# Cells over 24 feed-forward pieces each, and the last two groups of an mLSTM + feed-forward kernel in three float32r parts

## The chip, the cores and the metric

The kernel runs on one core of one Trainium2 chip. The metric is the device time of one execution in microseconds (us), the median of several runs. A core has TensorE (PE, with its weight loads shown apart as PEld), VectorE (DVE), ScalarE (ACT), GpSimd (POOL) and SyncE (SP), which here does nothing but issue DMA transfers. Each engine works through its own instructions in order and waits on semaphores for the others. The profile also shows the queues that issue, for instance SPq.

## The reference

Two blocks follow each other. The first is an mLSTM cell over 4 batches, 8 heads, 768 time steps and a head dimension of 40. The second takes its output as 3072 tokens of 320 numbers through a feed-forward layer of width 2048 with a leaky ReLU.

```python
for t in range(S):
    m_new = np.maximum(f_gate[:, :, t] + m, i_gate[:, :, t])
    f_stab = np.exp(f_gate[:, :, t] + m - m_new)
    i_stab = np.exp(i_gate[:, :, t] - m_new)
    m = m_new
    C = f_stab[..., None, None] * C + i_stab[..., None, None] * np.einsum('bhd,bhe->bhde', vt, kt)
    n = f_stab[..., None] * n + i_stab[..., None] * kt
    h_tilde = np.einsum('bhde,bhe->bhd', C, qt)
    denom = np.maximum(np.abs(nq), 1.0)          # nq = n . q
    y[:, :, t] = o * h_tilde / denom             # o = sigmoid(o_gate)
x = y.transpose(0, 2, 1, 3).reshape(B * S, H * D)
h = x @ w_in                                     # (3072, 320) @ (320, 2048)
return np.maximum(0.01 * h, h) @ w_out           # @ (2048, 320)
```

q, k, v and the gates are float32. w_in and w_out arrive in 64 bits per number, and the kernel turns them into float32 itself.

## The kernel before

**Chunks and groups.** The 768 time steps are cut into six chunks of 128, numbered 0 to 5. A step s is one chunk of one batch: s = 4 x chunk + batch, 24 in all. The recurrence inside a chunk is done with matrix products (scores under a causal mask, and a state per head that goes from chunk to chunk). Chunk g of all four batches gives 512 tokens, and these are group g of the feed-forward. Group g is computed while the cells of chunk g + 1 are computed, so that TensorE always has large matmuls between the small ones.

**A group's 32 pieces** (`ff_units`, L737). The first 16 are eight pairs: the first layer for two blocks of 128 hidden units, five slots of two matmuls (L743), one on the partitions 0 to 63 and one on 64 to 127, 512 columns each, in two PSUM tiles. A pair ends with two leaky ReLUs on ACT (L751), which write into `acts`. The last 16 pieces are the second layer: for each of four blocks of 128 tokens four pieces of four matmuls of 320 columns (L778), then a copy out of PSUM (L786) and an output DMA. All matmuls are float32. The first layer's PSUM tiles and the second layer's `po` share four banks (`psf`), the cells have the other four (`psc`).

**The cells of chunks 2 to 5.** A step has two visits on PE: `u_parts` (scores, and the chunk's addition to the state: L598, L603) and `u_mix` (output: L679). They come for two steps at a time. Behind `u_mix` DVE turns the result (L686), makes denominators, multiplies with the output gate (L690), POOL divides (L693), DVE turns back (L697), and SP stores x to `x_dr` in DRAM (L700). `gather_x` (L703) fetches it from there into `xT`, the input of the group's first layer, with four DMAs for each step. `ahead(s + 2)` then prepares the next step but one: DVE's `prep_kq` (L489, L495), POOL's `prep_vu` (L462) and `state_next` (L576), and SP's loads of k and q for two steps later. The decay matrix `w` is loaded (`spread`), gets the causal mask on POOL (`prep_mask`, L434), and its exponentials are taken on ACT (L442), three for each step in each piece, from three pieces after `ahead` on.

**What sets the order.** PE, DVE, ACT and POOL work in the order in which the program's text issues instructions. The main loop (L945) issues, for each piece, exponentials, masks, the piece, gates of the next chunk, the visits due after it, gathers and loads. `pairs` says after which of the 32 pieces the nine visits of a chunk come, `masks` before which pieces its masks:

```python
masks = {0: (2, 3), 12: (4, 5)}
pairs = (2, 2, 6, 6, 14, 14, 19, 19, 19)
```

SP's DMAs are ordered by the framework. Group 5 runs after the last cells, with nothing beside it.

**Loads of v.** For steps of chunk 1 on, four DMAs of 40 KB put v straight into the tile `S_t` of the batch, which also holds the batch's state (L343).

**Weights.** Eight pieces of w_in and w_out each are loaded in 64 bits and narrowed by `narrow_weights` (L220) on ACT and DVE during chunks 0 and 1. Pool `consts` holds them with all other constants for the whole kernel.

Of the kernel before, what the change touches and what calls it, by code (L numbers as in the profile page):

```python
# [9 lines left out]
F32 = mybir.dt.float32  # L10
U32 = mybir.dt.uint32
U64 = mybir.dt.uint64
AF = mybir.ActivationFunctionType
ALU = mybir.AluOpType
PSUM = bass.MemoryType.PSUM


@with_exitstack
def kernel(
# [28 lines left out]
    P = 128  # L48
# [22 lines left out]
    assert KR == DP and KC == 5 and KC * DP == Dm and GT * 4 <= 2048  # L71

    consts = ctx.enter_context(tc.tile_pool(name="consts", bufs=1))
    gp = ctx.enter_context(tc.tile_pool(name="gates", bufs=1))
    wk = ctx.enter_context(tc.tile_pool(name="wk", bufs=2))
    psf = ctx.enter_context(tc.tile_pool(name="psf", bufs=4, space=PSUM))
    psc = ctx.enter_context(tc.tile_pool(name="psc", bufs=4, space=PSUM))
# [47 lines left out]
    acts = consts.tile([P, NF, GT], F32, name="acts")  # L125
# [36 lines left out]
    QN = NF // 4  # L162
    QC = 4 * P
    WC = KC * 2 * P
    w_in = consts.tile([P, QN, WC], F32, name="w_in")
    w_out = consts.tile([P, NF, Dm], F32, name="w_out")
# [5 lines left out]
    def w_row(r, slot, j):  # L172
        n, e = divmod(j, 2)
        at = (2 * slot + e) * P
        return w_in[DP * r : DP * (r + 1), n, at : at + P]
# [6 lines left out]
    HW = 2 * Dm  # L182
    wide = moe_w_in.dtype == U64
    raws = {}
    if wide:
        raw_t = consts.tile([P, 5 * HW], U64, name="raw")

    def load_weights(n):

        m = n - QN  # L190
        if n < QN:
            dst = w_in[:, n, :]
        else:
            dst = w_out[:, 2 * m : 2 * m + 2, :].rearrange("p a d -> p (a d)")
        to = dst
        if wide:
            if n < 2:
                at = NF * GT - 2 * WC * (n + 1)
                raw = acts_l[:, at : at + 2 * WC].bitcast(U64)
            elif n < QN:  # L200
                raw = raw_t[:, WC * (n - 2) : WC * (n - 1)]
            elif m < 2:
                raw = w_out[:].rearrange("p f d -> p (f d)")[:, (2 + m) * WC : (3 + m) * WC].bitcast(U64)
            else:
                at = (4, 0, 1, 2, 3, 4)[m - 2] * HW
                raw = raw_t[:, at : at + HW]
            raws[n] = (raw, dst)
            to = raw
# [11 lines left out]
    def narrow_weights(n):  # L220
# [3 lines left out]
        if not wide:  # L224
            return
# [102 lines left out]
    def load(s):  # L328
# [12 lines left out]
        for u in range(2):  # L341
            for i in range(2):
                nc.sync.dma_start(  # L343
                    S_v[n][ts(u, SL), u, :, i, :DB],
                    v[b, :, c * P + u * SL : c * P + (u + 1) * SL, DB * i : DB * (i + 1)].rearrange("h p d -> p h d"),
                )
# [43 lines left out]
    def spread(s):  # L390

        c, b = divmod(s, B)
        d = st[s]
        w = wk.tile([P, H, P], F32, name="w", bufs=NL)
        d["w"] = w[:].rearrange("p h t -> p (h t)")[:, : H * SL].rearrange("p (h t) -> p h t", t=SL)
        for u in range(2):
            nc.sync.dma_start(d["w"][ts(u, SL)], a_dr[c, 0, u, b * H : (b + 1) * H, :].partition_broadcast(SL))
# [31 lines left out]
    def prep_mask(s):  # L429
        if s in masked:  # L430
            return
        masked.add(s)
        w = st[s]["w"]
        nc.gpsimd.tensor_tensor(w, w, cm2.unsqueeze(1).to_broadcast([P, H, SL]), op=ALU.add)  # L434
# [31 lines left out]
    def prep_qs(s):  # L466
# [3 lines left out]
        d["qs"] = wk.tile([P, Dm], F32, name="y")[:].rearrange("p (h d) -> p h d", d=D)  # L470
# [232 lines left out]
    def gather_x(s):  # L703

        c, b = divmod(s, B)
        if ("xT", c) not in st:
            st["xT", c] = wk.tile([P, KC, GT], F32, name="xT", bufs=1)
        xT = st["xT", c]
        src = x_dr[s].rearrange("(k p) t -> p k t", p=DP)
        for r in range(2):  # L710
            at = 0
            while at < KC:
                k0, n = run_of(r, at)
                nc.sync.dma_start(xT[DP * r : DP * (r + 1), at : at + n, ts(b, P)], src[:, k0 : k0 + 2 * n - 1 : 2, :])
                at += n

    def u_x(s):
# [3 lines left out]
        if b == 0:  # L721
            st["xT", c] = wk.tile([P, KC, GT], F32, name="xT", bufs=1)
# [14 lines left out]
    def ff_units(g):  # L737
# [36 lines left out]
        def part(n, m):  # L774
# [6 lines left out]
            if m == 3:  # L781
                if n < 2:
                    y = wk.tile([P, Dm], F32, name="y")[:]
                else:
                    y = wk.tile([P, H, D1], F32, name="hn")[:].rearrange("p h d -> p (h d)")[:, :Dm]
# [138 lines left out]
    with tc.manual_schedule(engines={E.PE, E.DVE, E.Activation, E.Pool}):  # L924
# [13 lines left out]
        ffs = ffs[2:]  # L938
# [3 lines left out]
        masks = {0: (2, 3), 12: (4, 5)}  # L942
        pairs = (2, 2, 6, 6, 14, 14, 19, 19, 19)
        now = (None for n in range(2, QN + NF // 2) for _ in narrow_weights(n))
        for c in range(1, NB + 1):  # L945
            if c > 1:
                ffs = ff_units(c - 1)
            cells = cell_units(c) if c < NB else []
            n_ff, n_c = len(ffs), len(cells)
            done = fed = 0  # L950
            waiting = []
            for i in range(n_ff):
                if c == 1:
                    run(now, 2 if i < 10 else 3 if i < 14 else 4)
                    for n in fetch.get(i, ()):
                        load_weights(QN + n)
                    if i == 0:
                        prep_mask(B)
                        ahead(B)
                        load_fi(3)  # L960
# [70 lines left out]
```

## Time and profile before

| what | us |
|---|---|
| median of three runs (527.24, 528.85, 529.04) | 528.85 |
| span of the profiled execution, first to last instruction | 526.4 |
| chunk 0 and group 0 with the cells of chunk 1 | 139.64 |
| group 1 with the cells of chunk 2 | 78.82 |
| group 2 with the cells of chunk 3 | 78.77 |
| group 3 with the cells of chunk 4 | 78.76 |
| group 4 with the cells of chunk 5 | 78.04 |
| group 5, first layer, then second layer | 34.53 + 34.74 |
| from the last matmul to the end | 3.1 |

The stages end where the chain of waits shows the next group's first matmul. The profile has only the span; the run's own time contains some time around it, and the median of the runs lies 2.45 us above the span. The TensorE clock in the profile is the one granted, as a share of the full one.

| engine | busy us | share of the span |
|---|---|---|
| PE | 513.2 | 97% |
| DVE | 240.3 | 46% |
| ACT | 168.1 | 32% |
| POOL | 113.0 | 21% |

Busy times are of the whole span; DVE, ACT and POOL are busy mostly in its first three quarters. "L743" is line 743 of the kernel before.

### The profile page before, as it was taken

To read this page: it belongs to the slowest core of one execution; us is meant where nothing else is said; L and a number is where in the kernel's file an instruction comes from. 1 tells how busy PE (TensorE), PEld (TensorE's weight loads), DVE (VectorE), ACT (ScalarE), POOL (GpSimd) and SP (SyncE) were. 2 spreads that over 40 slices of the span, in tenths; PEclk is the share of its full clock that TensorE was granted. 3 is DMA by queue.
4 is the path that set the end of the run, shared out by engine and by line. 5 is a ranking of instruction groups with operands and counts; after the bars stand their busy time and mean duration, and the time that the engine had idled before them with its cause. 6 is when DMAs were issued, how large, how long until landed. Compare 5 with 4: busy or idle time off the path is not lost.

```text
span 526.4 us, 11333 instructions
## 1 busy us (share of the span) xinstructions
PE 513.2 (97%) x4501; PEld 336.3 (64%) x4501; DVE 240.3 (46%) x431; ACT 168.1 (32%) x458; POOL 113.0 (21%) x145
## 2 busy tenths in 40 slices
PE   8889989999999999999999999999999999999997
PEld 7877878777555577555577555577554577544675
DVE  4679998999328446028445028344028230000000
ACT  4565865534534212034212124212125100122100
POOL 4244354152205121015021015021013010000000
PEclk9668999999999999999999999999999999999999
DMA  9977687888755626685626676626542112000000
GB/s 116 156 204 153 138 212 171 196 145 175 146 137 105 137 72 150 129 174 107 138 75 143 134 150 129 138 76 155 125 102 52 50 52 87 14 0 1 12 12 25
DMA packets 165284, 59.13 MB, mean 112 GB/s; under 512 B 128816, under 2 KB 156016, under 8 KB 165232
## 3 DMA queue, kind: packets, MB, share of 16 engines
q1 hardware_dynamic: 164848, 58.28, 51.0%
q8 instruction: 35, 0.57, 0.5%
q10 hardware_dynamic: 384, 0.13, 0.1%
q14 instruction: 17, 0.14, 0.1%
HBM read 51.68 MB, written 6.70 MB: 111 GB/s over the span
## 4 chain that ended last, share of the span: by engine, by line
PE 83%; SPq 6%; DVE 4%; DMA 2%; ACT 2%; issue 1%; POOL 1%; ACTq 0%; POOLq 0%
PE po L778 38%; PE ph L743 36%; PE pT L679 3%; SPq L213 3%; PE sd L598 3%; SPq L338 2%; SPq L352 1%; PE sd L603 1%; DMA rb<-in_q_dram 1%; DVE raw L245 1%; DVE qn L608 1%; DMA S<-in_v_dram 0%; DMA raw<-in_moe_w_in_dram 0%; PE tk L518 0%; PE hN L649 0%
## 5 line engine op out<-in xcount | busy, mean ns | idle before, releaser
L743 PE MATMUL ph<-xT,w_in 64*128 64x512 f32 (+1 forms) x1120 | 215.2, 536 | 0.6 <-ACT acts L751 0.6
L778 PE MATMUL po<-w_out,acts 128*128 128x320 f32 x768 | 211.1, 434 | 0.0
L778 PEld LDWEIGHTS po<-w_out,acts 128*128 128x128 f32 x768 | 144.5, 190 | 62.6 <-issue 4.1
L743 PEld LDWEIGHTS ph<-xT,w_in 64*128 64x128 f32 x1120 | 107.8, 189 | 94.4 <-issue 87.7
L751 ACT ACTIVATE acts<-ph 128x512 f32<-128x512 f32 (+1 forms) x112 | 53.9, 534 | 151.8 <-PE ph L743 151.7
L608 DVE TENSOR_TENSOR qn<-w,sd 64x512 f32<-64x512 f32 x40 | 27.4, 684 | 97.7 <-PE sd L603 57.1
L576 POOL TENSOR_TENSOR S<-S,f 40x336 f32<-40x336 f32 x36 | 30.9, 858 | 101.9 <-PE pT L679 65.8
L442 ACT ACTIVATE w<-w,gT 128x64 f32<-128x64 f32 (+1 forms) x192 | 51.1, 348 | 3.1 <-POOL w L434 2.1
L434 POOL TENSOR_TENSOR w<-w,i 128x512 f32<-128x512 f32 x20 | 28.1, 1411 | 104.7 <-ACT bu L294 53.0
L786 ACT COPY y<-po 128x320 f32<-128x320 f32 x12 | 5.1, 423 | 83.3 <-PE po L778 83.3
L786 ACT COPY hn<-po 128x320 f32<-128x320 f32 x12 | 5.1, 426 | 76.0 <-PE po L778 76.0
L686 DVE STREAM_TRANSPOSE hb<-pT 128x512 f32<-128x512 f32 x16 | 11.4, 714 | 39.2 <-PE pT L679 39.0
L495 DVE TENSOR_TENSOR qn<-kqT,ea 64x512 f32<-64x512 f32 x32 | 27.3, 854 | 0.9
L693 POOL TENSOR_TENSOR xb<-xb,den 128x320 f32<-128x320 f32 x16 | 11.7, 728 | 66.5 <-DVE xb L690 66.5
L598 PEld LDWEIGHTS sd<-kqT 40*64 40x64 f32 x640 | 19.9, 135 | 6.1 <-issue 6.1
L697 DVE STREAM_TRANSPOSE x<-xb 128x512 f32<-128x512 f32 x16 | 18.1, 1130 | 7.7 <-POOL xb L693 7.7
L598 PE MATMUL sd<-kqT 40*64 40x64 f32 x640 | 21.5, 220 | 0.0
L603 PE MATMUL sd<-S,vu 64*40 64x42 f32 x576 | 20.1, 214 | 0.7 <-POOL vu L462 0.7
L489 DVE STREAM_TRANSPOSE kqT<-rb 128x512 f32<-128x512 f32 x32 | 20.5, 677 | 0.0
L603 PEld LDWEIGHTS sd<-S,vu 64*40 64x40 f32 x576 | 18.6, 111 | 0.8 <-POOL vu L462 0.8
L580 DVE TENSOR_TENSOR S<-S,sd 40x336 f32<-40x336 f32 x36 | 18.1, 503 | 1.0
L679 PEld LDWEIGHTS pT<-qn,S 128*64 128x64 f32 x512 | 15.6, 138 | 3.6 <-issue 3.5
(126 smaller groups left out, 364.9 us busy)
## 6 DMA issues: line engine op xcount, KB each, us to landing
w<-a_dr SPq DMA_DIRECT2D x40, 128.0 KB
rb<-in_k_dram SPq DMA_DIRECT2D x64, 80.0 KB
rb<-in_q_dram SPq DMA_DIRECT2D x64, 80.0 KB
rb<-in_o_gate_dram SPq DMA_DIRECT2D x64, 80.0 KB
ea<-a_dr SPq DMA_DIRECT2D x32, 128.0 KB
kn<-in_k_dram SPq DMA_DIRECT2D x24, 160.0 KB
raw<-in_moe_w_out_dram SPq DMA_DIRECT2D x6, 640.0 KB
S<-in_v_dram SPq DMA_DIRECT2D x80, 40.0 KB
```

What stands on the lines that cost most here:

```text
L434: nc.gpsimd.tensor_tensor(w, w, cm2.unsqueeze(1).to_broadcast([P, H, SL]), op=ALU.add)
L442: yield nc.scalar.activation(w[:, h, :], w[:, h, :], AF.Exp, bias=gT[c][:, 0, bh : bh + 1], scale=1.0)
L489: nc.vector.transpose(d["kqT"][:, i].rearrange("p (h t n) -> p h n t", n=TS, t=QW), raw_blocks(s, i, QW).rearrange("p (h n) d -> p h n d", ...
L495: nc.vector.tensor_tensor(mixed(s)[rows, 1 - r], d["kqT"][rows, 1].rearrange("p (h t) -> p h t", t=SL), d["ea"][rows], op=ALU.mult,)
L576: nc.gpsimd.tensor_tensor(new, old, g, op=ALU.mult)
L598: nc.tensor.matmul(bank[1 - u][toks, h, :], lhsT=kqT[rows, 0, ts(h, SL)], rhs=kqT[rows, 1, ts(h, SL)], start=True, stop=True,)
L603: nc.tensor.matmul(dC[u][:, h].rearrange("p k d -> p (k d)"), lhsT=d["ku"][toks, h], rhs=S_v[s % NL][toks, u, h, :, :V1], start=True, stop ...
L608: nc.vector.tensor_tensor(mixed(s)[toks, u], w[toks], bank[1 - u][toks], op=ALU.mult)
L679: nc.tensor.matmul(pT[DP * r : DP * (r + 1), j * P + u * SL : j * P + (u + 1) * SL], lhsT=S[:, u, h, :], rhs=m[:, u, h, :], start=True, st ...
L743: nc.tensor.matmul(ph[r][:, cols], lhsT=w_row(r, slot, j), rhs=xT[DP * r : DP * (r + 1), slot, cols], start=(slot == 0), stop=(slot == KC ...
L751: nc.scalar.activation(acts[:, f, cols], ph[r][:, cols], AF.Prelu, alpha=0.01)
L778: nc.tensor.matmul(po[n][:], lhsT=acts[:, f, ts(n, P)], rhs=w_out[:, f, :], start=(f == 0), stop=(f == NF - 1),)
```

## The change

1. **Cells in 24 pieces.** Chunk 2 begins with piece 0 of group 1 as before, but each of the chunks 2 to 5 takes 24 pieces and not 32. The pieces are counted through over the groups 1 to 3, so a chunk's cells now run across the end of a group. Chunk 5 stops after its last visit (piece 18 of its 24), which leaves five pieces of group 3. The visits' places are 2, 7, 13, 18. The gathers of group 2 stand in pieces 20 to 23 of chunk 2, those of group 3 in pieces 2 to 5 of chunk 4.
2. **Masks and v.** The masks move to pieces 8 and 19, next to the visits. From chunk 2 on v comes in one DMA into the unused part of the step's `w` tile, and two POOL copies just ahead of the mask put it into `S_t`. The load of `w` is one DMA and not two.
3. **Three parts.** Groups 4 and 5 are cut into half-groups 8 to 11 of 256 tokens. Let h be a number with its low 12 bits cleared (`HIGH`) and l the rest. A weight w = h + l becomes three float32r tiles: h, 4096 l, and 4096 l - h. An x = H + L becomes H, L, and H / 4096 - L. One PSUM sum takes the products of the first and second parts, hH + 4096 lL, another those of the third parts. The first times 1 + 1/4096 plus the second is hH + hL + lH + lL, the whole product. So each float32 matmul becomes three float32r matmuls. `enter(u)` is the first layer of two blocks of hidden units (u counts eight in each half-group), and its sums are put together by ACT, DVE and ACT. `grow(u)` splits its result and `leave(u)` is the second layer, two u later. Half-group 8 has its second layer in float32 (`whole`), half-groups 9 to 11 have three parts.
4. **Where the splitting is done.** `split_w` splits 640 columns at a time on DVE, POOL, ACT and, one step later (`finish`), ACT and DVE. The first quarter of w_in is split during chunk 3, five of the remaining fourteen halves beside the last five pieces of group 3, and the others two at a time ahead of each `enter` of half-group 8. `split_x` splits x of a half-group in two steps.
5. **Memory.** The cells' pools are closed after chunk 5, and the parts take their place, also that of `acts`, `w_in`, `raw` and `w_out`. Outputs have two `y` tiles in place of two `y` and two `hn`.

The diff, cut to what the text speaks of:

```diff
+F32R = mybir.dt.float32r
+HIGH = 0xFFFFF000
+SPLIT = 4096.0
+JOIN = 1.0 + 1.0 / SPLIT
...
         nc.sync.dma_start(d["k"][:, :, :D], k[b, :, rows, :].rearrange("h p d -> p h d"))
+        w = wk.tile([P, H, P], F32, name="w", bufs=NL)[:].rearrange("p h t -> p (h t)")
...
+        d["v"] = w[:, H * SL : H * SL + Dm].rearrange("p (h k d) -> p h k d", k=2, d=DB)
+        nc.sync.dma_start(
+            w[:, H * SL : H * SL + Dm].rearrange("p (h d) -> p h d", d=D), v[b, :, rows, :].rearrange("h p d -> p h d"),
+        )
...
-        for u in range(2):
-            nc.sync.dma_start(d["w"][ts(u, SL)], a_dr[c, 0, u, b * H : (b + 1) * H, :].partition_broadcast(SL))
+        src = a_dr[c, 0, :, b * H : (b + 1) * H, :].rearrange("u h t -> u (h t)").unsqueeze(1).to_broadcast([2, SL, H * SL])
+        nc.sync.dma_start(d["w"].rearrange("p h t -> p (h t)"), src)
...
         w = st[s]["w"]
+        for u in range(2 if s >= 2 * B else 0):
+            nc.gpsimd.tensor_copy(S_v[s % NL][ts(u, SL), u, :, :, :DB], st[s]["v"][ts(u, SL)])
         nc.gpsimd.tensor_tensor(w, w, cm2.unsqueeze(1).to_broadcast([P, H, SL]), op=ALU.add)
...
-        masks = {0: (2, 3), 12: (4, 5)}
-        pairs = (2, 2, 6, 6, 14, 14, 19, 19, 19)
+        masks = {8: (2, 3), 19: (4, 5)}
+        pairs = (2, 2, 7, 7, 13, 13, 18, 18, 18)
+        UC = 24
...
+        def split_w(w, parts):
+            tmp = raw_b[:].bitcast(F32)
+            n = WC // 2
+            for i in range(2):
+                at = slice(n * i, n * (i + 1))
+                h, low = (tmp[:, n * (2 * i + k) : n * (2 * i + k + 1)] for k in range(2))
+                nc.vector.tensor_scalar(
+                    h.bitcast(U32), w[:, at].bitcast(U32), scalar1=HIGH, scalar2=None, op0=ALU.bitwise_and,
+                )
+                nc.gpsimd.tensor_tensor(low, w[:, at], h, op=ALU.subtract)
+                nc.scalar.copy(parts[0][:, at], h)
+                finish()
+                tail.append((parts, at, h, low))
+                yield
+
+        def finish():
+            for parts, at, h, low in tail:
+                nc.scalar.activation(parts[1][:, at], low, AF.Copy, scale=SPLIT)
+                nc.vector.scalar_tensor_tensor(
+                    parts[2][:, at], in0=low, scalar=SPLIT, in1=h, op0=ALU.mult, op1=ALU.subtract,
+                )
+            tail.clear()
...
+        for c in range(2, NB):
+            cells, done, fed = cell_units(c), 0, 0
+            for i in range(UC):
+                if at == len(ffs):
+                    g, at = g + 1, 0
+                    ffs = ff_units(g)
+                exponents()
+                for n in masks.get(i, ()):
...
+                if c == 3:
+                    if i == 2:
+                        now = split_in(0)
+                    if i in (3, 6, 9):
+                        run(now, 1)
+                ffs[at]()
...
+                visits(c, i)
+                if c == 2 and i >= UC - B:
+                    gather_x(2 * B + i - UC + B)
+                if c == 4 and 2 <= i < 2 + B:
+                    gather_x(3 * B + i - 2)
+                fetches()
+                if c == NB - 1 and i == pairs[-1]:
+                    break
...
+        load_x(HG0)
+        first = split_x(HG0)
+        now = splits()
+        while at < len(ffs):
+            ffs[at]()
+            at += 1
+            run(first, 1)
+            run(now, 1)
...
+        def enter(u):
...
+            ph = psh.tile([P, 2, 2, GH], F32, name="p3")
+            for v in range(3):
+                for slot in range(KC):
+                    for r in range(2):
+                        nc.tensor.matmul(
+                            ph[:, r, v // 2, :], lhsT=w[rows, v, c0 : c0 + P], rhs=x[v][rows, slot, :],
+                            start=(slot == 0 and v != 1), stop=(slot == KC - 1 and v != 0),
+                        )
+            nc.scalar.activation(a, ph[:, :, 0, :], AF.Copy, scale=JOIN)
+            nc.vector.tensor_tensor(a, a, ph[:, :, 1, :], op=ALU.add)
+            nc.scalar.activation(a, a, AF.Prelu, alpha=0.01)
...
+        def grow(u):
...
+            nc.vector.tensor_scalar(h.bitcast(U32), a.bitcast(U32), scalar1=HIGH, scalar2=None, op0=ALU.bitwise_and)
+            nc.scalar.copy(g[:, 0], h)
+            nc.vector.tensor_tensor(g[:, 1], a, h, op=ALU.subtract)
+            nc.vector.scalar_tensor_tensor(g[:, 2], in0=h, scalar=JOIN, in1=a, op0=ALU.mult, op1=ALU.subtract)
...
+        for u in range(HG0 * NJ, HG2 * NJ + LAG, 2):
+            hg, j = divmod(u, NJ)
+            for i in range(2):
+                if HG1 * NJ < u <= HG2 * NJ:
+                    grow(u - 2 + i)
+            for i in range(2):
+                if hg < HG1:
+                    run(now, 2)
+                if u < HG2 * NJ:
+                    enter(u + i)
+            if hg + 1 < HG2:
+                if j == 2:
+                    first = split_x(hg + 1)
+                if j in (2, 4):
+                    run(first, 1)
...
+            for i in range(2):
+                if u >= HG0 * NJ + LAG:
+                    leave(u - LAG + i)
```

`psh`, the PSUM of `enter`, has two buffers of two banks; `leave` adds up in two of two banks (`pso`).

## The prediction

> **What bounds the kernel now.** I read the page's busy times and slices first, then a table of stages, the chain that ended last, and the timelines of the engines that the change loads.
>
> ```profile
> span 526.4 us, 11333 instructions
> ...
> PE 513.2 (97%) x4501; PEld 336.3 (64%) x4501; DVE 240.3 (46%) x431; ACT 168.1 (32%) x458; POOL 113.0 (21%) x145
> ...
> PEclk9668999999999999999999999999999999999999
> ```
>
> PE is the bound, at full granted clock after the first fifth. Cut at the ends of the feed-forward groups, the stages are (columns: span, busy PE, PEld, DVE, ACT, POOL, clock, DMA share, GB/s):
>
> ```profile
> 139.64:218.46 78.82, 78.82 (x681) 47.83 (x680) 34.40 (x65) 20.30 (x60) 16.09 (x19) 1.00 0.53 122
> 297.23:375.99 78.76, 78.76 (x680) 47.77 (x680) 32.74 (x58) 20.29 (x60) 17.36 (x20) 1.00 0.59 131
> 375.99:454.03 78.04, 78.04 (x611) 47.09 (x610) 23.73 (x44) 15.62 (x40) 8.41 (x10) 1.00 0.26 64
> 454.03:488.56 34.53, 34.53 (x162) 15.40 (x161) 0.00 (x0) 8.03 (x15) 0.00 (x0) 1.00 0.02 6
> 488.56:523.30 34.74, 34.66 (x129) 24.17 (x128) 0.00 (x0) 2.37 (x6) 0.00 (x0) 1.00 0.04 14
> ```
>
> PE has no gap, DVE and POOL are idle in the last 69 us, and group 5 alone costs 34.53 (first layer) + 34.74 (second) = 69.3 us. So a group with its chunk's cells (78.8) holds 9.5 us of cells. The chain's end has the prices of a matmul:
>
> ```profile
> 454.03 34.53 PE ph L743 x160
> 488.56 34.66 PE po L778 x128
> 523.30 0.43 ACT hn L786
> ```
>
> Each float32 matmul is two records. One of 320 columns costs 2 x 34.66/128 = 542 ns; two row tiles of 512 columns cost 4 x 34.53/160 = 863 ns, or, with 256 columns (60 records in 6.68 us in the chain), 445 ns.
>
> **What the change removes.** Float32 in groups 4 and 5. A 24-bit product consists of four products of 12-bit halves; the mask HIGH leaves each part 12. So I price one part at a quarter of a float32 matmul, three at 3/4. No float32r row exists: the bounds are the quarter, and one record (half). I take the quarter, since the arithmetic fits it. First layer: 15 row-tile pairs x 445/4 = 1.67 us for each u, up to 1.74 if the per-record overhead (about 9 ns) stays whole; I take 1.70. Second layer: 12 x 542/4 = 1.63, taken 1.64. There are 32 u, 8 with a float32 second layer (4 x 0.542 = 2.17) and 24 with three parts: 32 x 1.70 + 8 x 2.17 + 24 x 1.64 = 111.1 us in place of 2 x 69.3 = 138.6. **-27.5 us.**
>
> [...] Here 128-row loads of 190 ns (L778) vanish inside records of 271 ns, so I charge none. [...]
>
> **Cells in 24 pieces.** A piece is 69.3/32 = 2.17 us. PE's cell work is the same; what matters is whether the others follow in 3/4 of the time. DMA: 0.59 x 78.8 = 46 us per chunk, less what v's halved packets save, in about 61.6: room. DVE 34 and POOL 17 + copies: room. Three places are tight; T is the start of a pair of u_mix.
>
> (a) The mask. Behind a pair of u_mix POOL runs state_next, xb, vu; in the timeline, from pT at 236.32, this ended at 248.38, T+12.1. Now four v copies and two masks follow, where before the masks had been made a pair earlier. A copy of 64x320 lies between 0.23 (64x64 copy, L149) and 0.72 us (320 columns, L462): taken 0.5. Masks are 2.95 us for two, so they end at T+17.0. The first exponentials need them, ACT takes them in order (12 in 2.97 us), and the relu of the piece queues behind: it ends about T+18.9 in chunk 2 (relu of pieces 10 and 11) and T+20.4 at the end of chunk 4 (pieces 6, 7 of group 3). PE wants those two PSUM buffers at T+17.1 and T+17.2: **+1.8, +3.2.** Elsewhere the piece is a second-layer one, or (c) covers it. Bounds 0 and 9.
>
> (b) Parts after six pieces: kqT of the second s was done at 249.0, T+12.7; PE asks at T+16. Hidden, 3 us spare.
>
> (c) The gather of group 2. SP's order:
>
> ```profile
> 274.23 1.46 SPq L700 DMA_DIRECT2D x_dr<-x  x4
> 281.87 1.66 SPq L700 DMA_DIRECT2D x_dr<-x  x4
> 288.63 5.16 SPq L714 DMA_DIRECT2D xT<-x_dr  x8
> ```
>
> With T = 269.17, x goes out at T+5.1 and the loads of the next pair end at T+19.4. The gather used to stand there; now o, k, v and w of two s come first (about 7.5 us from SP's rows of 0.4 to 0.65), then two outputs (0.9) and sixteen gathers of 0.66: T+38.4, and about 2 us to land. PE needs xT whole at piece 8 of chunk 3: T + 2.0 + 13 x 2.17 + 4.0 = T+34.3. **+6.1**, bounds 0 and 9. Group 3's gather has 20 us more and is hidden.
>
> **Costed at nothing.** split_in(0) in chunk 3 (two halves: DVE 2.6 us, POOL 3.2, ACT 1.6) hides beside PE, which has 61 us of work there; if POOL were late, the next masks would be. The second pair of output tiles goes: a y tile is wanted again two units of 8.7 us later, and its output issues in 0.4 us; were it late, ACT's copy and the relus behind it would wait. load_x of half-groups 9 to 11 takes SP 5.2 us in a half-group of 27 us, when nothing else is loaded; were it late, DVE would stand with grow behind it. Splitting x (POOL 3.2, DVE 2.6 us per half-group) hides likewise.
>
> **The seam.** After the last u_mix pair only five pieces of group 3 remain; then u = 64 starts. Before that x and the weights are split, in order, on DVE, POOL and ACT. DVE is free 9.0 us after T0:
>
> ```profile
> 425.91 2.08 PE L679 MATMUL pT<-qn,S 128*64 128x64 f32 x64
> 433.81 1.10 DVE L697 STREAM_TRANSPOSE x<-xb 128x512 f32<-128x512 f32 x1 [0.84 <-POOL xb L693]
> ```
>
> In enter's order, the ACT and DVE steps that empty u = 64's PSUM stand behind the pieces of split_w before them, up to the sixth half emitted there (w_in 3, second). That is, on POOL, 768 + 512 + 6 x 640 columns at 1.27/512 = 12.7 us; on DVE masks (0.49 per 640) and scalar_tensor_tensors (0.82 per 640), 10.5 us. Do they run beside each other? Rows:
>
> ```profile
> 109.03 1.19 POOL L462 TENSOR_TENSOR vu<-kn,gT 128x320 f32<-128x320 f32 x1
> 247.66 0.72 POOL L462 TENSOR_TENSOR vu<-kn,gT 128x320 f32<-128x320 f32 x1
> ```
> ```profile
> 112.07 1.27 DVE L241 SCALAR_TENSOR_TENSOR w_out<-raw,w_out 128x640 uint32<-128x640 uint32 x1
> 125.95 0.82 DVE L241 SCALAR_TENSOR_TENSOR w_out<-raw,w_out 128x640 uint32<-128x640 uint32 x1
> ```
>
> From 106.4 to 113.9 both were busy, and did in 7.5 us what takes 9.4 apart: a rate of 1.25. So 23.2/1.25 = 18.6 us, to T0+27.6; then scalar_tensor_tensor, add (0.68, L608) and ACT's steps, 2.1: u = 66 starts at T0+29.7. PE has been through five pieces (T0+12.9), 1.3 of waiting for POOL's part of x and two enters at T0+17.6: it stands 12.1 us. u = 67 waits for two more halves (4.6 - 1.7 = 2.9). **+16.3**; with no interference +9, with none side by side +22.
>
> [...]
>
> While PE stands its clock may fall: it was 0.50 in 24.7 to 31.5, after early gaps. One 3.4 us stretch at half speed behind the gather, **+1.7** (0 to 4). At the seam the second wait covers it.
>
> **End.** The last sum needs an add (336 columns took 0.50, L580) after ACT's copy: **+0.5.**
>
> **Sum.** -27.5 + 1.8 + 3.2 + 6.1 + 16.3 + 1.7 + 0.5 = +2.1 on the profiled span of 526.4, so 528.5. The runs' median (528.85) is 2.45 above that span; I carry this over: **531 us**. Within 0.5% of before is 526.2 to 531.5, about what the runs can tell from no change.
>
> **Rivals.**
> - Smaller waits. If POOL and DVE do not slow each other (seam +9), and SP and the masks cost half (5.5): -27.5 + 9 + 5.5 + 0.5 = -12.5, **516 us**. For it: 21% POOL, 46% DVE. Against: 1.19 beside 0.72.
> - Slower: DVE becomes the bound behind the seam. Two u take PE 6.7 us. DVE needs two adds (0.68), two masks (0.39 for 512), two subtractions and two scalar_tensor_tensors (0.66 each): 4.8, and 1.6 or 1.1 where x is split. With two PSUM buffers each late add delays the u after next; it decides once DVE's round passes 6.7, which 6.4 nearly does. At 1 us per round in the last 12 rounds: **543 us**.
> - A float32r part costs one record: 15 x 223 and 12 x 271 ns, 32 x 3.34 + 17.3 + 24 x 3.25 = 202 us, +91: **622 us**. With the waits above there is nothing left to pay even a small surcharge over the quarter.
>
> **How the numbers follow.** Forecast 0.47 (523 to 540), smaller waits 0.28, DVE 0.18, one record 0.07. The forecast's terms can shift by several us, so of its 0.47 I put 0.10 below 526.2, 0.17 within, 0.20 above. Faster 0.10 + 0.28 = 0.38; same 0.17; slower 0.20 + 0.18 + 0.07 = 0.45. Range 512 to 547: it takes in the seam's bounds, most of the smaller waits and of the DVE case, and leaves the one-record case and the ends out.
>
> **What would show it.** Records of 256 columns with about 110 ns per pair and of 320 with about 137; PE idle near 12 us behind u = 65, released by DVE's add; PE waiting 6 us on a DMA of xT at group 2's start; relus behind exponentials that wait for POOL's mask; hardly a gap in the last 80 us. I am wrong if the seam's halves take 1.6 us and not 2.3, if xT lands in time, or if the last three half-groups have gaps each round.

## The result: 590.9 us, 11.7% slower

The changed kernel takes 590.85 us (median of four runs, 588.5 to 592.1), the kernel before 528.94 on the same chip. The ratio is 1.117, with a 95% interval of 1.113 to 1.121. The forecast was 531, its range 512 to 547: the change costs 62 us and not 2. The profiled execution of the changed kernel has a span of 590.3 us, 63.9 more than that of before.

The page of the changed kernel, busy times and the clock in 40 slices:

```profile
span 590.3 us, 13125 instructions
...
PE 518.9 (88%) x5237; PEld 391.1 (66%) x5237; DVE 358.8 (61%) x589; ACT 228.4 (39%) x554; POOL 178.8 (30%) x201
...
PEclk9659996999799899959999999899996799999999
```

PE was busy for 97% of the span and is now at 88%: 71 us without a matmul, in place of 13. Its clock also falls again and again. Cut into stages (columns: stage, span, busy PE, PEld, DVE, ACT, POOL, clock, DMA share, GB/s), the changed kernel shows where. The stages are: to the first matmul of group 1; groups 1, 2 and 3, in which all cells of chunks 2 to 5 now lie; the seam, to where PE no longer waits; the rest.

```profile
0.00:161.60 161.60, 135.27 (x1572) 110.74 (x1572) 113.29 (x200) 79.47 (x214) 53.69 (x79) 0.86 0.71 152
161.60:262.89 101.29, 86.75 (x871) 53.62 (x871) 44.63 (x79) 25.49 (x74) 25.90 (x31) 0.92 0.40 97
262.89:346.41 83.52, 83.52 (x807) 54.54 (x807) 48.85 (x84) 24.28 (x76) 32.12 (x41) 0.98 0.55 131
346.41:437.13 90.72, 83.57 (x681) 54.62 (x680) 42.18 (x76) 21.20 (x59) 22.78 (x29) 0.96 0.46 114
437.13:482.94 45.81, 26.58 (x213) 21.93 (x212) 38.41 (x38) 26.12 (x42) 33.93 (x17) 0.78 0.09 25
482.94:586.28 103.34, 103.18 (x1100) 95.67 (x1100) 70.80 (x114) 51.40 (x91) 10.42 (x5) 1.00 0.07 21
```

The first stage of the kernel before, for comparison:

```profile
0.00:139.57 139.57, 129.53 (x1571) 106.18 (x1572) 115.10 (x200) 80.77 (x217) 53.79 (x76) 0.91 0.83 166
```

The first row is the surprise. Up to group 1 nothing of the parts has begun and no cell has moved; only the load of `w`, the output tiles and the places in memory differ, and yet the stage takes 161.6 us in place of 139.6. In the last row PE has no gap: there the float32r parts run as planned. Between them lie gaps in group 1 (14.5 us), in group 3 (7.2) and at the seam (19.2).

The waits of the changed kernel by engine (columns: total us, times, longest):

```profile
PE p L1165 <- DVE xa L1170: 13.8, 3, 10.5
PE ph L767 <- DMA xT<-x_dr: 12.9, 1, 12.9
PE ph L767 <- ACT xT L753: 10.1, 1, 10.1
PE ph L767 <- ACT acts L775: 8.8, 2, 7.2
PE tk L539 <- DMA rb<-in_q_dram: 8.5, 2, 7.4
...
ACT y L807 <- DMA out_dram<-y: 28.4, 3, 15.0
...
SPq L403 <- DMA w<-a_dr: 9.4, 3, 4.5
...
SPq L731 <- DMA w<-a_dr: 6.0, 2, 3.1
```

The gather of xT, the relus and the seam were foreseen, though smaller. Three things were not. SP itself waits for the landing of `w`. ACT waits 28 us for output DMAs. And PE waits in the first 160 us for loads that were on time before. Four rows of the chain show such landings:

```profile
87.44 7.47 DMA rb<-in_q_dram
...
126.25 11.73 DMA raw_a<-in_moe_w_out_dram
...
153.23 7.51 DMA out_dram<-y
...
245.01 10.73 DMA w<-a_dr
```

The last row is the load of one step's decay matrix, which is now one DMA. The trace's records of single packets say more: its 128 packets of 2 KB start over 6.3 us, at 100 ns each, so on the average 128 x 0.100/6.3 = 2.0 of them are under way at once. In the kernel before, the same 128 packets in two DMAs start over 1.9 to 2.0 us at 130 to 145 ns each (the loads at 222 and 229 us): by the same sum, about 9 at once.

### The profile page after: what moved, and what is told of

Its sections match the earlier page's. It is cut to its first block, busy times and chain, and to the rows that moved or that the text cites. A ratio compares the mean times of both kernels' runs of the same rounds, so it can differ in the third digit from the quotient of the medians.

```text
span 590.3 us, 13125 instructions
## 1 busy us (share of the span) xinstructions
PE 518.9 (88%) x5237; PEld 391.1 (66%) x5237; DVE 358.8 (61%) x589; ACT 228.4 (39%) x554; POOL 178.8 (30%) x201
## 4 chain that ended last, share of the span: by engine, by line
PE 50%; DVE 17%; DMA 11%; SPq 11%; ACT 4%; issue 4%; POOL 2%; ACTq 0%; DVEq 0%; POOLq 0%
PE ph L767 19%; PE po L802 11%; PE so L1204 8%; PE p L1165 6%; DVE raw_b L977 3%; SPq L228 3%; SPq L403 2%; DMA raw_a<-in_moe_w_out_dram 2%; DMA w<-a_dr 2%; SPq L351 2%; PE sd L619 2%; DMA rb<-in_q_dram 2%; PE pT L700 2%; DMA rb<-in_o_gate_dram 1%; DMA out_dram<-y 1%
## 5 line engine op out<-in xcount | busy, mean ns | idle before, releaser
L767 PE MATMUL ph<-xT,w_in 64*128 64x512 f32 (+1 forms) x800 | 154.7, 535 | 31.7 <-DMA xT<-x_dr 12.9
L767 PEld LDWEIGHTS ph<-xT,w_in 64*128 64x128 f32 x800 | 90.2, 199 | 87.3 <-issue 44.2
L802 PE MATMUL po<-w_out,acts 128*128 128x320 f32 x512 | 142.8, 436 | 0.7 <-DVE w_out L260 0.7
L802 PEld LDWEIGHTS po<-w_out,acts 128*128 128x128 f32 x512 | 95.7, 190 | 41.1 <-issue 1.8
L1165 PE MATMUL p<-xs,wi 64*128 64x256 f32 x960 | 67.3, 297 | 19.2 <-DVE xa L1170 13.8
L1165 PEld LDWEIGHTS p<-xs,wi 64*128 64x128 f32 x960 | 63.2, 200 | 24.3 <-DVE xa L1170 14.7
L775 ACT ACTIVATE acts<-ph 128x512 f32<-128x512 f32 (+1 forms) x80 | 36.3, 506 | 70.0 <-PE ph L767 69.9
L1204 PE MATMUL so<-wo,g 128*128 128x320 f32 x288 | 45.5, 314 | 0.1
L1204 PEld LDWEIGHTS so<-wo,g 128*128 128x128 f32 x288 | 42.3, 188 | 2.1 <-DVE g L1187 0.3
L1127 POOL TENSOR_TENSOR xs<-xa,xh 128x768 fp32r<-128x768 f32 (+1 forms) x8 | 17.3, 2166 | 62.3 <-DVE xh L1125 62.3
L807 ACT COPY y<-po 128x320 f32<-128x320 f32 x16 | 6.7, 416 | 59.7 <-DMA out_dram<-y 28.4
```

Source lines behind the costliest of these rows:

```text
L767: nc.tensor.matmul(ph[r][:, cols], lhsT=w_row(r, slot, j), rhs=xT[DP * r : DP * (r + 1), slot, cols], start=(slot == 0), stop=(slot == KC ...
L775: nc.scalar.activation(acts[:, f, cols], ph[r][:, cols], AF.Prelu, alpha=0.01)
L802: nc.tensor.matmul(po[n][:], lhsT=acts[:, f, ts(n, P)], rhs=w_out[:, f, :], start=(f == 0), stop=(f == NF - 1),)
L1165: nc.tensor.matmul(ph[:, r, v // 2, :], lhsT=w[rows, v, c0 : c0 + P], rhs=x[v][rows, slot, :], start=(slot == 0 and v != 1), stop=(slot == ...
L1204: nc.tensor.matmul(p[:, v // 2, :Dm], lhsT=lhsT, rhs=rhs, start=(j == 0 and r == 0 and v != 1), stop=(j == NJ - 1 and r == 1 and (whole or ...
```

## The experiments

I held these theories. A: the one DMA for `w` keeps only two of the 16 DMA engines at work (an estimate from the 2.0 packets), and everything that has a share on those two is late. B: two output tiles in place of four make ACT wait. C: 24 pieces are too few for SP and POOL, whatever the DMA. At the seam, D: POOL's subtraction holds up DVE, against E: the mask is slow by itself.

### w in two DMAs again

```diff
-        src = a_dr[c, 0, :, b * H : (b + 1) * H, :].rearrange("u h t -> u (h t)").unsqueeze(1).to_broadcast([2, SL, H * SL])
-        nc.sync.dma_start(d["w"].rearrange("p h t -> p (h t)"), src)
+        for u in range(2):
+            nc.sync.dma_start(d["w"][ts(u, SL)], a_dr[c, 0, u, b * H : (b + 1) * H, :].partition_broadcast(SL))
```

> The changed kernel with the decay matrix w loaded in two DMAs of 64 rows, as before, and not in one. Theory A (the one DMA is worked off by two of the 16 DMA engines: its 128 packets of 2 KB come within about 6 us in place of 2, and what stands behind them on these two engines is late): group 1 starts near 141 us in place of 161.6, group 1 takes about 85 in place of 101.3 (78.8 and the gather's 6), groups 2 and 3 lose some 8 of their waits; in all about 548 us in place of 590.9. Theory B (two output tiles, ACT's copy waits for the output DMA): those waits stay, at most 10 us are gained, 580. Theory C (24 pieces are too few for SP and POOL): the start recovers (-20), the waits behind it stay, 569.

Measured: 563.6 us, ratio 1.067 (1.064 to 1.070), 27 us less than the changed kernel. Its stages (to group 1, group 1, the seam) and one of its waits:

```profile
0.00:143.66 143.66, 129.56 (x1572) 105.74 (x1572) 115.78 (x200) 79.48 (x214) 56.34 (x79) 0.93 0.82 170
143.66:239.54 95.88, 86.95 (x870) 53.59 (x871) 44.47 (x79) 25.37 (x74) 25.90 (x31) 0.95 0.42 104
...
409.23:455.25 46.02, 26.90 (x215) 22.16 (x214) 38.61 (x39) 26.15 (x43) 34.13 (x17) 0.78 0.08 25
```

and in the list of waits

```profile
ACT y L807 <- DMA out_dram<-y: 18.8, 3, 7.4
```

The start is nearly whole again (143.7), and the seam has not moved. But group 1 still takes 95.9 and not 85, and ACT still waits for its output tiles. A is the largest cause, not the only one.

### The same DMA in the kernel before

The kernel before with the edit above turned round, and nothing else:

```diff
-        for u in range(2):
-            nc.sync.dma_start(d["w"][ts(u, SL)], a_dr[c, 0, u, b * H : (b + 1) * H, :].partition_broadcast(SL))
+        src = a_dr[c, 0, :, b * H : (b + 1) * H, :].rearrange("u h t -> u (h t)").unsqueeze(1).to_broadcast([2, SL, H * SL])
+        nc.sync.dma_start(d["w"].rearrange("p h t -> p (h t)"), src)
```

> The kernel before with one edit: w in one DMA. Theory A: the first 140 us, in which the DMA engines are busy for about three quarters of the time, become some 20 us longer, and the later chunks, where w is fetched half a chunk ahead, hide it: about 549 us. Theories B and C: nothing but the landing of w itself is later, 529 to 532.

Measured: 556.1 us, ratio 1.053 (1.050 to 1.057). One DMA in place of two makes the kernel before 28 us slower, as much as its removal gave. Its first stage, and below it PE's waits:

```profile
0.00:155.42 155.42, 131.88 (x1571) 106.99 (x1571) 115.19 (x200) 80.93 (x217) 52.10 (x76) 0.90 0.70 149
```

```profile
PE tk L518 <- DMA rb<-in_q_dram: 8.8, 2, 4.7
PE ph L743 <- DMA xT<-x_dr: 6.6, 2, 4.1
PE po L778 <- DVE w_out L247: 5.1, 1, 5.1
```

The start grows by 16 us. The chunks behind it lose the other 11; I had expected them to hide it.

### Two DMAs, cut the other way

```diff
-        for u in range(2):
-            nc.sync.dma_start(d["w"][ts(u, SL)], a_dr[c, 0, u, b * H : (b + 1) * H, :].partition_broadcast(SL))
+        for i in range(2):
+            h = slice(b * H + i * H // 2, b * H + (i + 1) * H // 2)
+            src = a_dr[c, 0, :, h, :].rearrange("u h t -> u (h t)").unsqueeze(1).to_broadcast([2, SL, H // 2 * SL])
+            nc.sync.dma_start(d["w"][:, i * H // 2 : (i + 1) * H // 2, :].rearrange("p h t -> p (h t)"), src)
```

> The kernel before with one edit: w still comes in two DMAs, but each brings four heads for all 128 rows (outermost dimension 2, as in the one DMA of the change) where before each brought all heads for 64 rows. Theory A in its exact form (the outermost dimension sets how many DMA engines work, here two): the packets of 1 KB again come over 5 us or more and the kernel is about as slow as with one DMA, 550 to 556 us. Rival: one DMA of 256 KB is the matter, not its shape; two DMAs of half the size then cost what they did before, 528 us.

Measured: 570.3 us, ratio 1.079 (1.075 to 1.083), above the 550 to 556 expected. So it is not the size of the DMA, nor that there is one. With the outermost dimension 2, even two DMAs are slow: their 256 packets of 1 KB start over 6.8 us at 53 ns each, 256 x 0.053/6.8 = 2.0 at once. They are 14 us slower than the one DMA; that the smaller packets are the reason is likely, but not shown. PE's waits in this run:

```profile
PE tk L520 <- DMA rb<-in_q_dram: 15.1, 2, 10.6
PE ph L745 <- DMA xT<-x_dr: 13.8, 2, 7.2
PE po L780 <- DVE w_out L247: 7.1, 1, 7.1
```

So in two shapes of the load with 2 outermost 2.0 packets are under way at once, and with 64 rows outermost about 9. That it is always the same two engines is not seen in these traces, which do not name a packet's engine, but it would explain why other loads are so late.

### Four output tiles

```diff
-                y = fp.tile([P, Dm], F32, name="y", bufs=2)[:]
+                if n < 2 or g > 2:
+                    y = fp.tile([P, Dm], F32, name="y", bufs=2)[:]
+                else:
+                    y = wk.tile([P, H, D1], F32, name="hn")[:].rearrange("p h d -> p (h d)")[:, :Dm]
```

> As two_spreads, and the outputs of groups 1 and 2 in four tiles, two y and two hn, as before. Theory B: at least 10 us less than two_spreads. Theory A: less than 3 us of difference, since the output DMAs were late only behind the slow w.

Measured: 556.1 us, ratio 1.056 (1.050 to 1.062), 7.5 us below two_spreads by the medians; the profiled executions differ by 1.6 only, so the size is uncertain. ACT's waits for output DMAs are gone from the list. So is one gap of PE: in two_spreads PE stands 3.8 us at 139.8, just ahead of group 1, behind an ACT copy that waits for an output tile. B is a cause of some 2 to 9 us, between both expectations. PE's two largest waits in the cells are now the two that the prediction had:

```profile
PE ph L767 <- DMA xT<-x_dr: 7.5, 1, 7.5
PE ph L767 <- ACT acts L775: 5.5, 3, 3.3
```

### Gather earlier, exponentials later

```diff
-                late[s] = 3
+                late[s] = 4
...
-                if c == 2 and i >= UC - B:
-                    gather_x(2 * B + i - UC + B)
+                if c == 2 and i in (16, 17, 20, 21):
+                    gather_x(2 * B + (16, 17, 20, 21).index(i))
```

> As two_spreads_hn, with two edits in the cells: the gathers of group 2's first two steps stand in pieces 16 and 17 of chunk 2, ahead of the next loads, and the exponentials of a step start four pieces behind its preparation and not three. If SP's order makes xT late and the masks make the relus late, as predicted, PE's wait for xT falls from 7.5 us to 2 or 3 and its waits for relus from 5.5 to about 1; with less idling the clock dips less (3 us): 556 - 12 = 544 us. Rival: the later exponentials hold up the scores' product with w instead, and half of it comes back: 550.

Measured: 542.9 us, ratio 1.029 (1.027 to 1.031), as expected. The waits fell from 7.5 to 1.4 and from 5.5 to 1.9 us, and with no long gap the clock stays at full speed:

```profile
138.57:222.98 84.41, 83.02 (x872) 51.64 (x871) 45.19 (x80) 24.72 (x70) 26.20 (x32) 1.00 0.50 124
222.98:304.78 81.80, 81.80 (x806) 50.69 (x807) 48.50 (x84) 24.45 (x75) 31.88 (x41) 1.00 0.62 145
304.78:388.22 83.44, 81.55 (x679) 50.05 (x678) 41.61 (x74) 21.28 (x59) 22.60 (x29) 1.00 0.48 115
```

The three groups take 249.6 us in place of 266.4 in two_spreads_hn. 9.2 of these 16.8 us are gaps (12.5 to 3.3); the rest is the clock: in two_spreads_hn PE did 15.7 us of its work in these groups at half speed, in eased none. C falls: 24 pieces are enough, if the order on SP and POOL is right.

### The cells alone

The cells of the kernel above, and groups 4 and 5 in float32 behind them, with no part and no split; all six groups use four output tiles.

```diff
-        cell.close()
...
+        while g < NB:
+            if at == len(ffs):
+                g, at = g + 1, 0
+                if g == NB:
+                    break
+                ffs = ff_units(g)
+            ffs[at]()
+            at += 1
+            if g == NB - 2 and 16 <= at < 16 + B:
+                gather_x((NB - 1) * B + at - 16)
```

> Part 1 and 2 of the change alone: the cells as in eased, groups 4 and 5 in float32 as before, with nothing beside them. The cells' work on PE is only moved, so without the late DMAs and masks it costs what its waits cost: 138.6 to the start of group 1, 249.7 for groups 1 to 3 (of eased), 2 x 69.3 for groups 4 and 5 and 3.2 at the end, 530 of span, 532 us; before plus 3. Rival: with no DVE and POOL work beside groups 4 and 5 PE runs faster than the sum, and the cells in 24 pieces alone are a gain.

Measured: 531.75 us, ratio 1.0075 (1.006 to 1.009); span 530.5. The sum holds to half a microsecond. Cells in 24 pieces gain nothing and cost 4 us: 2.4 of gaps, and 2 of longer PE work in the cells, whose cause is open.

### The seam: subtraction on DVE

```diff
-                nc.gpsimd.tensor_tensor(low, w[:, at], h, op=ALU.subtract)
+                nc.vector.tensor_tensor(low, w[:, at], h, op=ALU.subtract)
```

> As two_spreads_hn, with the subtraction of split_w on DVE in place of POOL. Theory D (DVE's mask of 640 columns takes 1.65 to 1.74 us at the seam and 0.49 elsewhere because POOL's subtraction beside it holds it up): the mask falls to 0.49, a half costs DVE 0.49 + 0.75 + 0.74 = 2.0 us in place of 2.45, and 14 halves gain about 6 us: 550. Rival E (the mask is slow for another reason, its operands or its place): it stays at 1.65, a half costs DVE 3.1 us, and the seam grows by 9 us: 565.

Measured: 554.5 us, ratio 1.052 (1.048 to 1.056), against 556.1; the medians hardly tell the two apart, the traces do. First the timelines of DVE and of POOL in the changed kernel (columns: start, duration, engine, line, operation):

```profile
443.62 0.81 DVE L989 SCALAR_TENSOR_TENSOR wi<-raw_b 128x640 fp32r<-128x640 f32 x1
444.54 1.66 DVE L977 TENSOR_SCALAR raw_b<-w_in 128x640 uint32<-128x640 uint32 x1
446.12 0.81 DVE L989 SCALAR_TENSOR_TENSOR wi<-raw_b 128x640 fp32r<-128x640 f32 x1
```

```profile
443.84 2.00 POOL L980 TENSOR_TENSOR raw_b<-w_in,raw_b 128x640 f32<-128x640 f32 x1 [0.49 <-DVE raw_b L977]
```

Then DVE in the experiment:

```profile
412.35 0.49 DVE L980 TENSOR_SCALAR raw_b<-w_in 128x640 uint32<-128x640 uint32 x1
412.95 0.83 DVE L983 TENSOR_TENSOR raw_b<-w_in,raw_b 128x640 f32<-128x640 f32 x1
413.69 0.82 DVE L992 SCALAR_TENSOR_TENSOR wi<-raw_b 128x640 fp32r<-128x640 f32 x1
414.54 0.49 DVE L980 TENSOR_SCALAR raw_b<-w_in 128x640 uint32<-128x640 uint32 x1
```

The mask falls to 0.49: D holds and E falls. In the changed kernel the mask starts at 444.54, POOL's subtraction ends at 445.84, and the mask goes on to 446.20: 0.36 of its 0.49 us come behind POOL's end, so it hardly moved while POOL worked. POOL's subtraction takes 2.00 there. It starts 0.22 us behind DVE's scalar_tensor_tensor and ends 1.41 us behind that one's end. In chunk 3 two subtractions started ahead of it, and there it is the scalar_tensor_tensor that takes 2.15 in place of 0.82 (two_spreads_hn):

```profile
218.62 3.23 POOL L983 TENSOR_TENSOR raw_b<-w_in,raw_b 128x640 f32<-128x640 f32 x2 [7.58 <-DVE raw_b L980]
220.39 2.15 DVE L992 SCALAR_TENSOR_TENSOR wi<-raw_b 128x640 fp32r<-128x640 f32 x1 [1.44 <-POOL raw_b L983]
```

So in these rows the one that starts second waits for most of the other's time. A half takes 446.12 - 443.62 = 2.50 us in all; its operations one after the other would take 0.49 + 0.82 + 1.6 = 2.9, with a subtraction at 3.23/2 = 1.6. So the pair gains a factor of 1.16, some 0.1 to 0.2 us at each change from one engine to the other (0.49 - 0.36 and 1.6 - 1.41), where I took 1.25. With all three on DVE a half takes 414.54 - 412.35 = 2.19 us, less than the two engines need together. The seam, from the last piece of group 3 to the enter of u = 70, goes from 45.9 us in two_spreads_hn to 42.0: 4 us and not 6.

### The seam: nothing ahead of half-group 8

```diff
+            if hg < HG1:
+                for slot in range(KC):
+                    c0 = (2 * slot + e) * P
+                    for r in range(2):
+                        rows = slice(DP * r, DP * (r + 1))
+                        nc.tensor.matmul(
+                            ph[:, r, 0, :], lhsT=w_in(q)[rows, c0 : c0 + P], rhs=x8[rows, slot, :],
+                            start=(slot == 0), stop=(slot == KC - 1),
+                        )
+                nc.scalar.activation(a, ph[:, :, 0, :], AF.Prelu, alpha=0.01)
+                return
...
-                if hg < HG1:
-                    run(now, 2)
                 if u < HG2 * NJ:
                     enter(u + i)
+                if hg < HG1:
+                    run(now, 1 + i if u + i + 1 < HG1 * NJ else 4)
```

x8 is the x of half-group 8, fetched in piece 14 of chunk 5.

> As eased, with half-group 8 in float32 in both layers, so that the weights are split beside 46 us of plain matmuls and not ahead of them; the subtraction stays on POOL. Its x is fetched during chunk 5. If the seam's cost is that nothing runs beside the splitting, its some 20 us of idling and the slow clock behind it go (25 us), and the first layer of half-group 8 costs 8 x (2.23 - 1.9) = 2.7 us more: 544 - 22 = 522 us, faster than before. Rival: DVE needs 14 x 2.5 + 3 = 38 us for the splits and the prelus on ACT stand behind them in order, so that 8 to 10 us of waiting stay: 531, no gain.

Measured: 523.6 us, ratio 0.993 (0.991 to 0.995). In this run x of half-group 10 was loaded over x8 too early, so the last two u of half-group 8 worked on other numbers; the work and its order are the same. The next run loads it two u later:

```diff
-                if j == 4 and hg + 2 < HG2:
+                if j == 4:
                     run(first, 1)
+                if j == (6 if hg < HG1 else 4) and hg + 2 < HG2:
                     load_x(hg + 2)
```

> As hg8_f32, but x of half-group 10 is fetched two u later, behind the last product of half-group 8 that reads the same tile. SP has 20 us for it, so the time stays at 523 to 524 us, below before by 0.5 to 1%. Against cells_only it shows what the parts of half-groups 9 to 11 are worth: 3 x (34.6 - 30.0) = 13.9 us by the sum of the records, less what is left of the seam (2 to 4). Rival: the later load reaches the split of x late and DVE holds up the next half-group by 3 us or more.

Measured: 524.35 us, ratio 0.9943 with an interval of 0.9925 to 0.9961: faster than the kernel before by 0.6%, and than the changed kernel by 66 us. Its span and busy times, and its stages of half-group 8 and of the rest:

```profile
span 521.8 us, 13000 instructions
...
PE 504.8 (97%) x5157; PEld 373.9 (72%) x5157; DVE 353.9 (68%) x577; ACT 223.0 (43%) x544; POOL 176.9 (34%) x199
```

```profile
388.52:422.03 33.51, 31.85 (x208) 23.82 (x208) 31.06 (x26) 21.10 (x34) 26.77 (x14) 1.00 0.12 37
422.03:518.57 96.54, 95.09 (x1025) 89.06 (x1024) 70.27 (x113) 49.81 (x88) 11.07 (x6) 1.00 0.06 20
```

The splits now run beside plain matmuls (DVE 31 and POOL 27 us of these 33.5), and PE waits 1.7 us there. Against cells_only the three half-groups in parts gain 530.5 - 521.8 = 8.7 us of span, of the 13.9 that the records alone give and below the 10 to 12 expected; 3.1 of the missing 5.2 are the gaps in these two rows (1.66 and 1.45).

### What a float32r part is made of

```diff
+                        cut = Dm // 2 if v == 1 else Dm
                         nc.tensor.matmul(
-                            p[:, v // 2, :Dm], lhsT=lhsT, rhs=rhs,
+                            p[:, v // 2, :cut], lhsT=lhsT, rhs=rhs[:, :cut],
```

> As two_spreads, but the second of the three parts of the second layer (4096 l times L) takes 160 of the 320 output columns in half-groups 9 to 11; so the other half of that small product is left out of the output. It asks what the 155 ns of a 320-column part are made of. If a part is as long as its weight load (128 columns of weights), the 24 records of two u stay at 3.71 us and nothing changes. If it is columns at the full clock (133 ns) and about 20 ns for itself, 8 of the 24 fall to 87 ns, two u to 3.17 us, and the run is 6.5 us shorter than two_spreads.

Measured: the 24 records of two u take 3.43 us, between the two expectations; the one run took 562.65 us. A row of its chain:

```profile
536.03 3.43 PE so L1205 x24
```

In the trace's single records, parts of 320 columns start 147 ns apart in two_spreads. Here, a short part and the two long ones around it take 74 + 184 + 149 = 407 ns in place of 441: the part behind the short one starts early and then lasts longer. The 128 x 128 weight loads of these parts never start closer than 108 ns to each other. I read this so: a part of 320 columns is set by its columns, with about 12 ns above the quarter of a float32 matmul (542/4 = 135), and the weight loads, never closer than 108 ns, set it only for the part of 160 columns. What the 12 ns are is open. The 133 ns in the expectation stand in no row; the float32 rows of before, 512 columns against 320, give (863 - 542)/192 x 320/4 = 134.

## Why the prediction was wrong, point by point

The spans in one table (us; stages as above):

| kernel | to group 1 | groups 1 to 3 | behind them | span |
|---|---|---|---|---|
| changed kernel | 161.6 | 275.5 | 153.1 | 590.3 |
| two_spreads | 143.7 | 265.6 | 153.0 | 562.3 |
| two_spreads_hn | 141.3 | 266.4 | 152.9 | 560.7 |
| eased | 138.6 | 249.6 | 153.0 | 541.2 |
| cells_only | 139.3 | 249.6 | 141.6 | 530.5 |
| hg8_late_x | 139.2 | 249.4 | 133.3 | 521.8 |

From 526.4 it is + 4.1 to cells_only, + 48.2 for what is late in the first two columns (161.6 + 275.5 against 388.9), and + 11.5 behind them: 590.2. The forecast had 0, + 12.8 (1.8 + 3.2 + 6.1 + 1.7) and - 10.7 (16.3 + 0.5 - 27.5). Row by row, 27.8 of the 48.2 go with the shape of `w` and 1.6 with the output tiles. 19.5 lie between two_spreads_hn and eased: 16.8 with the gather, the masks and the clock behind their waits, for which the forecast had the 12.8, and 2.7 ahead of group 1, which the edits do not touch. Eased lies 0.7 below cells_only.

**The step that failed most: "DMA: room".** I compared the mean share of 16 engines with the time of a chunk, and the DMA for `w` got no price, although the change lists it. The mean says nothing of a load of which only 2.0 packets are under way at once. In the first 140 us of the kernel before the DMA share was 0.83 already, and the changed kernel issues eight of these loads up to 153 us, each with its packets spread over 5.3 us or more. Taking the shape back gave 27 us, putting it into the kernel before cost 28: shown from both sides.

**"Costed at nothing": the second pair of output tiles.** The prediction named what would happen if an output were late: ACT's copy and what stands behind it would wait. That came. In two_spreads ACT's copy of an output of group 0 ends at 135.1, but SP, busy with the next steps' loads, issues its DMA only at 139.9. That lands at 142.8, and ACT waits 5.3 us and PE 3.8 for it. Cost 2 to 9 us. In the changed kernel the same wait comes on top of the slow `w` and PE stands 10.1 us. The rest of ACT's waits for outputs (18.9 of 28.4 us there, 13.5 of 18.8 in two_spreads) lies in the second half of group 1, around PE's wait for xT, and shows no wait of PE of its own.

**(a) and (c), masks and gather.** Predicted 5.0 and 6.1; once the DMA is mended, 5.5 and 7.5 (two_spreads_hn), each with the releaser named. The waits for the relus come where they were said: 1.6 us in chunk 2 (said 1.8) and 3.3 at the end of chunk 4 (said 3.2). Right. Under the slow DMA they were 8.8 and 12.9.

**The clock.** Predicted one stretch of 3.4 us (before's record of the granted clock changes in multiples of 3.41) and 1.7 us of loss. In the changed kernel's record of the granted clock, half speed begins 2.0 to 3.6 us behind the start of each gap of 4.5 us or more (7.4, 10.1, 12.9, 7.2, 4.5 and 10.5 us, at 87.5, 151.5, 250.0, 362.5, 437.7 and 448.3) and lasts 3 to 6 us beyond its end, which loses 1.4 to 2.9 us each time. The price of one gap was right; I charged for one, and there were six, and two more such stretches behind gaps of 1.6 and 2.2 us. PE was busy at half speed for 56 us in the changed kernel and for 21 in the kernel before, so that by this sum the clock costs 17.5 us more and not 1.7. From two_spreads_hn to eased this share is 16.8 - 9.2 = 7.6 us.

**(b)** had no wait in the list. Right.

**A float32r part.** Predicted 1.70 per u for the first layer, 1.64 for the second, 2.17 for the float32 second layer. The chain of the changed kernel, two u in each row:

```profile
491.36 3.79 PE p L1165 x60
495.15 4.50 PE so L1204 x16
...
503.45 3.71 PE so L1204 x24
```

These are 1.895, 1.855 and 2.25. A pair of 256 columns takes 3.79/30 = 126 ns (said: about 110), a part of 320 columns 3.71/24 = 155 with the change between the layers in it (said: 137). So the quarter was the right end of the bounds, and three parts cost 0.85 of a float32 matmul, not 0.75. Over 32 u that is 123.2 us in place of 111.1, and the gain 15.4 in place of 27.5. So the step was right and its size was off by 12 us; no row of before could have given it. The bounds reached to 202, and I took the value next to their lower end.

**The end.** Said + 0.5; the changed kernel ends 4.0 us behind its last matmul, in place of 3.1.

**The seam.** Predicted 12.1 + 2.9 + 1.3 = 16.3. Measured: gaps of 4.5, 10.5, 2.2, 1.0 and 1.1, and with the slow clock the stage takes 45.8 us for 3 x 3.79 + 2 x 4.50 = 20.4 us of work: 25.4 lost, 19.2 in gaps and 6 to the clock. Right were the place, the releaser (DVE's add) and DVE's end with the cells (said T0 + 9.0, measured T0 + 8.7). Four sizes were off. DVE then waits 2.8 us for the DMA that stores x; the split itself reads the x of another chunk, so I take the reason to be its tile, which lies in memory of the closed cells:

```profile
435.50 0.56 DVE L1125 TENSOR_SCALAR xh<-xa 128x768 uint32<-128x768 uint32 x1 [2.77 <-DMA x_dr<-x]
```

Next, the combined rate of 1.16 in place of 1.25 is worth 23.2/1.16 - 23.2/1.25 = 1.4 us. The waits do not end with u = 67: u = 69 and 70 wait 2.0 us more, as DVE needs two halves and an add for each u. And the slow clock behind the gaps, which I had set to nothing here, takes some 3 us: of its 6, 2.9 fall on the first two u, ahead of the 10.5 us in which PE waits for DVE anyway. That makes 9.2 for the 9.1 missing; the division among the four is mine, from the gaps and durations, and only the slowing of the mask was tested by itself. Why the stretch of before overlapped better is open.

**The rivals.** Smaller waits: no. DVE as the bound in the last three half-groups: no. From 529.7 to 549.3 the chain runs through DVE, but PE has 0.2 us of gaps in that whole stage; DVE follows at 70.8 of 103.3 us. One record for a part: no, 126 against 445 and 155 against 542 are 0.28 and 0.29. The weight loads, which the prediction charged with nothing, are 188 ns long and start every 147 ns beside the matmuls (two_spreads). Even if the 12 ns of a part were theirs, 288 parts (24 u of 12) would make 3.5 us.

## What to carry to other kernels

Before merging two DMAs, look at the outermost dimension of the new one: with 2 there these loads had only 2.0 packets under way at once, which cost 27 to 42 us in three comparisons, and the DMA share on the page, a mean over 16, does not show it. A split into cheaper parts has to be paid before the first part can run; it gained nothing until half a group of plain matmuls ran beside it. And a term whose price no row of the profile shows should not enter next to the better end of its bounds when the whole gain hangs on it: here that took 12 of the 27.5 us.

## What the runs showed of the hardware

- Of the load of `w`, 2.0 packets are under way at once in a DMA with outermost dimension 2, and about 9 for the same bytes in two DMAs with 64 rows outermost (two loads of the kernel before).
- Float32r matmuls of 320 columns start 147 ns apart, each with its own 128 x 128 weights; such a weight load can start 108 ns behind the last one.
- DVE's mask of 640 columns takes 0.49 us alone and 1.66 where a POOL subtraction has started before it; a scalar_tensor_tensor goes from 0.82 to 2.15 in the same way, and the subtraction from about 1.6 to 2.00 where DVE started first. Giving POOL's part to DVE was faster (2.19 in place of 2.50 us for a half).
